# Key rows loaded plainly and transposed on TensorE, w1 loaded whole, and abs-max scans moved by one query block in a fused attention and MLP kernel

## Chip, cores and metric

One core of one Trainium2 chip. The metric is device time of one execution in microseconds (us). All arrays are bf16. Times are medians of several executions of a compiled kernel; the profile is a separate, recorded execution, whose span can differ from the median by some us.

## The reference, cut to what matters

```python
# x: [1, 2048, 576]; k_cache, v_cache: [1, 16, 2048, 128]; wq: [576, 4096]; wo: [4096, 576]
# w1, w2: [576, 576]; w3: [576, 4608]; w4: [4608, 576]
def reference(x, k_cache, v_cache, wq, wo, w1, w2, w3, w4):      # batch and head axes cut
    xn = layernorm(x)
    # attention: 32 query heads share 16 key heads, only the last W = 512 keys of 2048
    q = (xn @ wq) per head;  k, v = the last W keys and values, each used by two heads
    s = softmax(q @ k.T * 128**-0.5) @ v, heads joined, @ wo
    # gate branch on the same xn
    h  = gelu(layernorm(xn) @ w1)
    hs = (the four column quarters of h, shifted by +1, -1, +2, -2 rows) @ w2
    x1 = xn + hs
    g  = silu(x1 + gelu(layernorm(x1) @ w3) @ w4)
    return x + s * g
```

## The kernel before, the parts that matter

The attention part walks over 128 units, four query blocks of 512 rows times 32 heads, which the text calls block 0 to 3 and head 0 to 31. TensorE, the transfer issues on SyncE and the issues on GpSimd are in program order. In each unit TensorE gets the scores of this head, the query product of the next one, the value product of the one before, and a third at a time "atoms" of other work: gate-branch products (`b1` in heads 15 to 19, `b2` with the shifted `hs`) and the output product of the previous block. `at(u, ...)` hangs loads and VectorE work on a unit. The w3/w4 stage after unit 127 isn't touched.

```python
def load_kv(g, eng=None):          # keys are transposed on the way by the DMA, on SyncE's queue
    nc.sync.dma_start(out=kT[:, g, :], in_=A_k_cache[0, g, K0:, :], transpose=True)
    (eng or nc.gpsimd).dma_start(out=v_sb[:, g, :, 0:Dh],
        in_=A_v_cache[0, g, K0:, :].rearrange("(kc p) d -> p kc d", p=P))

def load_w1():                     # 4 x 4 = 16 issues on GpSimd
    for g in range(4):
        nc.gpsimd.dma_start(out=w1_sb[:, 0:NF, g * P:(g + 1) * P], ...)
        ...                        # cut: three more of this kind

def load_wo(i):                    # 4 loads of 1152 KB
    h0 = i * 8
    nc.gpsimd.dma_start(out=wo_sb[:, h0:h0 + 8, :], ...)

def transpose_tile(dstT, src, tt): # xnnT and xT_b are made by DMA transposes on SyncE's queue, too
    nc.sync.dma_start(out=dstT[:, :, tt * P:(tt + 1) * P], in_=src[:, tt, :], transpose=True)

def stage_t(u):                    # and so is oT, once per head, from one of 4 o buffers
    ...
    last_t[0] = nc.sync.dma_start(out=oT[:], in_=o[:].rearrange("p a b -> p (a b)"), transpose=True)

def gelu1(b, c, ph):               # VectorE steps of the gate's GELU; only the first has priority
    x = g1_pool.tile([P, QB], BF16, name="g_x")
    with tc.high_priority(offset=HP):
        nc.vector.tensor_copy(out=x[:], in_=ph[:, :])
    ...                            # cut: five more VectorE steps and a tanh on ScalarE

for b in range(NB):
    base = b * Hq
    later(base + 7, lambda b=b: ln2_steps(b), 3)                 # second layernorm -> xnn
    for tt in range(TB):
        at(base + 10 + tt, lambda b=b, tt=tt: tr2(b, tt))        # its 4 transposes -> xnnT
    for c in range(5):
        pe(base + 15 + c, b1(b, c))                              # needs xnnT
    ...
    if b + 1 < NB:
        later(base + 24, lambda b=b: ln1_steps(b + 1), 3)        # layernorm of the next block
        for tt in range(TB):
            at(base + 27 + tt // 2, lambda b=b, tt=tt: tr1(b + 1, tt))   # -> xT_b of the next block
at(2, lambda: late(..., load_w1))
for i in range(4):
    at(4 + 6 * i, lambda i=i: late(..., lambda: load_wo(i)))
for g in range(Hkv):
    if g + 3 < Hkv:
        at(2 * g + 1, lambda g=g: load_kv(g + 3))
for j in range(2, NB * 8):
    at(4 * (j - 1) - 1, lambda j=j: load_wq(j))                  # wq for four heads
for j in range(8):                                               # 40 abs-max scans, in block 1
    for kc in range(NDC):
        at(Hq + 4 * j + (kc + 1) // 2, lambda j=j, kc=kc: wq_max(j, kc))
```

Of the kernel before, what the change touches and what calls it, by code (L numbers as in the profile page):

```python
# [8 lines left out]
P = 128  # L9
# [20 lines left out]
def kernel(  # L30
# [131 lines left out]
    with ExitStack() as actx:  # L162
# [10 lines left out]
        w1_sb = res.tile([P, NDC, 5 * P], BF16, name="w1_sb")  # L173
# [39 lines left out]
        def load_kv(g, eng=None):  # L213
            nc.sync.dma_start(out=kT[:, g, :], in_=A_k_cache[0, g, K0:, :], transpose=True)
            (eng or nc.gpsimd).dma_start(out=v_sb[:, g, :, 0:Dh], in_=A_v_cache[0, g, K0:, :].rearrange("(kc p) d -> p kc d", p=P))
# [15 lines left out]
        with tc.manual_schedule(engines={SP}):  # L231
            load_wq(0, nc.sync)
            load_kv(0, nc.sync)
            load_kv(1, nc.sync)
            load_wq(1, nc.sync)
            load_kv(2, nc.sync)
        nc.gpsimd.memset(v_sb[:, :, :, Dh:VW], 1.0)
        nc.gpsimd.memset(w1_sb[:, :, 4 * P:], 0.0)
# [3 lines left out]
        def load_wo(i):  # L242
            h0 = i * 8
            nc.gpsimd.dma_start(out=wo_sb[:, h0:h0 + 8, :],
                                in_=A_wo[h0 * P:(h0 + 8) * P, :].rearrange("(h p) d -> p h d", p=P))

        def load_w1():
            for g in range(4):
                nc.gpsimd.dma_start(out=w1_sb[:, 0:NF, g * P:(g + 1) * P],
                                    in_=B_w1[0:NF * P, g * c4:g * c4 + P].rearrange("(kc p) m -> p kc m", p=P))  # L250
                nc.gpsimd.dma_start(out=w1_sb[0:DR, NF, g * P:(g + 1) * P],
                                    in_=B_w1[NF * P:D, g * c4:g * c4 + P])
                nc.gpsimd.dma_start(out=w1_sb[:, 0:NF, 4 * P + 32 * g:4 * P + 32 * g + rsz],
                                    in_=B_w1[0:NF * P, g * c4 + P:(g + 1) * c4].rearrange("(kc p) m -> p kc m", p=P))
                nc.gpsimd.dma_start(out=w1_sb[0:DR, NF, 4 * P + 32 * g:4 * P + 32 * g + rsz],
                                    in_=B_w1[NF * P:D, g * c4 + P:(g + 1) * c4])
# [140 lines left out]
        def b1(b, c):  # L397
            st = {}

            def mm(kc):  # L400
# [8 lines left out]
                nc.tensor.matmul(st["ph"][:, :], lhsT=w1_sb[:, kc, c * P:(c + 1) * P], rhs=xnnT[:, kc, :],  # L409
# [6 lines left out]
        def gelu1(b, c, ph):  # L416
            hb = hb_t[b]
            x = g1_pool.tile([P, QB], BF16, name="g_x")
            with tc.high_priority(offset=HP):
                nc.vector.tensor_copy(out=x[:], in_=ph[:, :])  # L420
# [67 lines left out]
        def finish_flag():  # L488
# [4 lines left out]
            m1 = small.tile([1, 2, P], FP32, name="m1", bufs=1)  # L493
            nc.gpsimd.dma_start(out=m1[:], in_=mx_dram[:, :].rearrange("(o p) c -> o c p", o=1))
            mm = small.tile([1, 2], FP32, name="mm", bufs=1)
            nc.vector.tensor_reduce(out=mm[:], in_=m1[:], axis=AX.X, op=ALU.max)
# [53 lines left out]
        for i in range(4):  # L550
            at(4 + 6 * i, lambda i=i: late(pT_t[4 + 6 * i][0][0:1, 0:1], lambda: load_wo(i)))
        at(Hq + 4, lambda: late(pT_t[Hq + 4][0][0:1, 0:1], load_w2))
        for g in range(Hkv):
            if g + 3 < Hkv:
                at(2 * g + 1, lambda g=g: load_kv(g + 3))
            at(Hq + 2 * g + 1, lambda g=g: k_max(g))
        for j in range(2, NB * 8):
            at(4 * (j - 1) - 1, lambda j=j: load_wq(j))
        for j in range(8):
            for kc in range(NDC):  # L560
                at(Hq + 4 * j + (kc + 1) // 2, lambda j=j, kc=kc: wq_max(j, kc))
# [3 lines left out]
        at(2 * Hq + 4, finish_flag)  # L565

        with tc.manual_schedule(engines={SP, POOL, PE}):
            for step in ln1_steps(0):
                step()
            for _ in range(2):  # L570
                wu = ps_sc.tile([P, QB], FP32, name="warm", tag="sc")
                for i in range(24):
                    nc.tensor.matmul(wu[:, 0:P], lhsT=ident[:, :], rhs=ident[:, :], start=True, stop=True)
# [266 lines left out]
```

## Time and profile before

| kernel before | |
|---|---|
| time, first timing | 886.71 us (886.49 to 887.57, 3 executions) |
| span of the profiled execution | 887.6 us |
| busy: TensorE, ScalarE, VectorE, GpSimd | 96%, 51%, 44%, 10% |
| block 0, 1, 2: first query to first query of the next | 119.6, 141.4, 133.8 us |
| first query of all | 13.9 us after the start |

How to read it: TensorE has hardly any idle time left, so the share of busy time says little. What says more is the rhythm of the heads. Undisturbed heads of block 0 start their query product every 2.88 us, those with five more gate products every 3.96 us. Whatever an interval is longer than that is lost, whether TensorE stood still or ran at a lower clock after it. The lines that carry this are in the prediction below.

### The profile page before, as it was taken

What the parts mean: (1) busy time and instruction counts of PE and PEld (TensorE: products, weight loads), DVE (VectorE), ACT (ScalarE), POOL (GpSimd) and SP (SyncE); (2) the same over time, 40 slices, a digit from 0 to 9 for tenths busy, and PEclk for the clock granted to TensorE, in tenths of its full rate; (3) what the DMA queues carried; (4) which work ended last, traced back from release to release, by engine and by line L of the source; (5) the groups of instructions that cost most, each with busy time, mean ns of one, the idle gap of its engine ahead of it and who ended that gap; (6) DMA issues with size and microseconds to landing.
All of it is one profiled execution on the core that took longest, in us unless ns stands there. A gap on an engine that the chain in (4) does not pass through costs nothing.

```text
span 887.6 us, 16225 instructions
## 1 busy us (share of the span) xinstructions
PE 853.2 (96%) x6460; PEld 473.6 (53%) x6460; DVE 387.7 (44%) x1201; ACT 455.2 (51%) x814; POOL 86.1 (10%) x148
## 2 busy tenths in 40 slices
PE   7896989999899999999999999999999999999996
PEld 4463555566455466565466565454444444444454
DVE  4584873258985135873125865300044007005033
ACT  2673774378777359877359876032233224225510
POOL 2722210211001021010001001000000000000000
PEclk7997999999999999999999999999999999999999
DMA  6698691246227146246127235990005004001001
GB/s 127 149 210 174 137 191 51 57 98 125 63 81 129 39 99 124 70 112 105 40 68 144 76 90 120 320 311 20 1 27 137 1 1 149 16 1 54 1 17 42
DMA packets 145873, 83.73 MB, mean 94 GB/s; under 512 B 113408, under 2 KB 139392, under 8 KB 145792
## 3 DMA queue, kind: packets, MB, share of 16 engines
q1 hardware_dynamic: 133840, 52.16, 27.9%
q0 software_dynamic: 8544, 27.23, 11.0%
q10 hardware_dynamic: 3408, 3.25, 1.1%
q8 instruction: 52, 0.85, 0.4%
q14 instruction: 29, 0.24, 0.1%
HBM read 47.07 MB, written 9.44 MB: 64 GB/s over the span
## 4 chain that ended last, share of the span: by engine, by line

## 5 line engine op out<-in xcount | busy, mean ns | idle before, releaser
L322 ACT ACTIVATE pT<-sc 128x512 bf16<-128x512 f32 x512 | 289.7, 596 | 122.8 <-PE sc L320 114.7
L320 PE MATMUL sc<-qT,kT 128*128 128x512 bf16 x512 | 184.2, 384 | 1.0 <-DVE qT L310 0.9
L645 PE MATMUL ph<-xT_b,w_s 128*128 128x512 bf16 x720 | 172.1, 379 | 0.0
L305 PE MATMUL psq<-xT_b,wq_b 128*128 128x512 bf16 x640 | 164.0, 388 | 7.4 <-DMA wq_b<-in_A_wq_dram 3.8
L337 PEld LDWEIGHTS <-pT 128*128 128x128 bf16 x2048 | 141.1, 98 | 53.9 <-issue 3.0
L648 ACT ACTIVATE h<-ph 128x512 bf16<-128x512 f32 x144 | 85.8, 597 | 155.4 <-PE ph L645 151.1
L337 PE MATMUL po<-v_sb,pT 128*128 128x129 bf16 x2048 | 163.4, 222 | 0.7 <-ACT pT L322 0.4
L654 PE MATMUL pm<-w_s,h 128*128 128x512 bf16 x540 | 145.8, 380 | 0.0
L665 DVE TENSOR_TENSOR bs<-pm,x 128x512 f32<-128x512 f32 (+3 forms) x18 | 11.1, 630 | 246.6 <-PE pm L654 198.6
L341 DVE RECIPROCAL ri<-po 128x2 f32<-128x2 f32 x256 | 42.5, 166 | 173.8 <-PE po L337 170.8
L361 PE MATMUL pswo<-wo_sb,oT 128*128 128x512 bf16 x512 | 116.5, 379 | 0.0
L342 DVE TENSOR_TENSOR o<-po,ri 128x256 bf16<-128x256 f32 x256 | 107.5, 420 | 6.7 <-DMA oT<-o 1.0
L305 PEld LDWEIGHTS <-wq_b 128*128 128x128 bf16 x640 | 63.1, 99 | 86.7 <-issue 11.4
L645 PEld LDWEIGHTS <-w_s 128*128 128x128 bf16 x720 | 63.8, 98 | 73.4
L655 PE MATMUL pr<-w_s,h 128*128 128x64 bf16 x540 | 99.1, 193 | 0.0
L361 PEld LDWEIGHTS <-oT 128*128 128x128 bf16 x1024 | 65.0, 98 | 55.1
L654 PEld LDWEIGHTS <-h 128*128 128x128 bf16 x540 | 52.7, 98 | 63.9 <-issue 0.6
L312 ACT ACTIVATE qT<-psq 128x512 bf16<-128x512 f32 x96 | 57.4, 598 | 32.5 <-PE psq L305 32.4
L320 PEld LDWEIGHTS <-kT 128*128 128x128 bf16 x512 | 47.6, 98 | 30.3 <-issue 3.2
L655 PEld LDWEIGHTS <-h 128*128 128x128 bf16 x540 | 51.0, 98 | 12.2 <-issue 0.4
L209 POOL DMA_DIRECT2D wq_b<-in_A_wq_dram x30 | 23.3, 778 | 327.2 <-PE psq L305 254.4
L409 PE MATMUL ph<-xnnT,w_sb 128*128 128x512 bf16 x100 | 32.5, 390 | 8.7 <-DMA xnnT<-xnn_b 8.7
(88 smaller groups left out, 472.4 us busy)
## 6 DMA issues: line engine op xcount, KB each, us to landing
wq_b<-in_A_wq_dram POOLq DMA_DIRECT2D x30, 512.0 KB, 4.9
w_s<-in_B_w_dram SPq DMA_DIRECT2D x9, 576.0 KB, 8.1
wo_sb<-in_A_wo_dram POOLq DMA_DIRECT2D x4, 1152.0 KB, 7.4
w_s<-in_B_w_dram SPq DMA_DIRECT2D x9, 512.0 KB, 9.3
x_dram<-x SPq DMA_DIRECT2D x4, 576.0 KB, 3.4
x<-x_dram SPq DMA_DIRECT2D x4, 576.0 KB, 4.7
s_b<-s_dram SPq DMA_DIRECT2D x4, 576.0 KB, 6.5
x_b<-in_A_x_dram SPq DMA_DIRECT2D x4, 576.0 KB, 6.2
```

Of the source, the lines that this page charges most:

```text
L305: nc.tensor.matmul(psq[:, :], lhsT=w[:, kc, hh * Dh:(hh + 1) * Dh], rhs=xT_b[qb % 2][:, kc, :], start=(kc == 0), stop=(kc == NDC - 1))
L312: nc.scalar.activation(out=qT[:, :], in_=psq[:, :], func=ACT.Copy)
L320: nc.tensor.matmul(sc[:, :], lhsT=kT[:, g, kc * P:(kc + 1) * P], rhs=qT_t[u][:, :], start=True, stop=True)
L322: nc.scalar.activation(out=pT[:, :], in_=sc[:, :], func=ACT.Exp, scale=SCALE)
L337: nc.tensor.matmul(po[:, j, :], lhsT=pTs[kc][:, tt * P:(tt + 1) * P], rhs=v_sb[:, g, kc, 0:Dh + 1], start=(kc == 0), stop=(kc == KCH - 1))
L341: nc.vector.reciprocal(out=ri[:], in_=po[:, :, Dh])
L342: nc.vector.tensor_tensor(out=o[:, t0:t0 + 2, :], in0=po[:, :, 0:Dh], in1=ri[:].unsqueeze(2).to_broadcast([P, 2, Dh]), op=ALU.mult)
L361: nc.tensor.matmul(ps, lhsT=oT_t[qb * Hq + h][:, tt, :], rhs=wo_sb[:, h, lo:hi], start=(h == 0), stop=(h == Hq - 1))
L645: nc.tensor.matmul(ph[:, :], lhsT=w3[:, kc, f0:f0 + P], rhs=xT_b[b % 2][:, kc, :], start=(kc == 0), stop=(kc == NDC - 1))
L648: nc.scalar.activation(out=h3[:, :], in_=ph[:, :], func=ACT.Gelu_apprx_tanh)
L654: nc.tensor.matmul(pm[tt][:, :], lhsT=lhsT, rhs=w4[:, fc % WS, 0:M0], start=(fc == 0), stop=(fc == FC - 1))
L655: nc.tensor.matmul(pr[:, tt, :], lhsT=lhsT, rhs=w4[:, fc % WS, M0:D], start=(fc == 0 and tt == 0), stop=(fc == FC - 1), skip_group_check=True)
```

## The change

Its intent is to take the waits out of block 0 and of the stretch of block 1 where VectorE is late.

- **Keys.** Four key heads come in one plain load. With key `4p + kc` on partition `p`, each partition reads 1 KB in one piece instead of 256 B rows. The values get the same order of keys, so the sum over the keys is unchanged. TensorE transposes them (4 instructions per key head into PSUM) and VectorE copies them out.
- **w1** comes in 2 issues instead of 16; four VectorE copies gather the odd columns later.
- **wo** comes in 8 loads of 576 KB instead of 4 of 1152 KB.
- **The 40 scans** of wq go from block 1 to block 2; all GELU steps of VectorE get priority.

```diff
-        def load_kv(g, eng=None):
-            nc.sync.dma_start(out=kT[:, g, :], in_=A_k_cache[0, g, K0:, :], transpose=True)
-            ...
+        def load_k(i, eng=None, step=4):
+            kst_t[i] = x1_pool.tile([P, TB, D], BF16, name="x1")
+            ...
+                    in_=A_k_cache[0, 4 * i + g:4 * i + g + step, K0:, :].rearrange("g (p kc) d -> p g (kc d)", p=P))
+        def prep_k(g):
+            ...
+                nc.tensor.transpose(out=st["ps"][:, kc * P:(kc + 1) * P], in_=src[:, kc * P:(kc + 1) * P],
+                                    identity=ident[:, :])
+                if kc == KCH - 1:
+                    with tc.high_priority(offset=HP):
+                        nc.vector.tensor_copy(out=kT[:, g, :], in_=st["ps"][:, :])
         def load_w1():
+            nc.gpsimd.dma_start(out=w1_sb[:, 0:NF, :], in_=B_w1[0:NF * P, :].rearrange("(kc p) m -> p kc m", p=P))
+            nc.gpsimd.dma_start(out=w1_sb[0:DR, NF, :], in_=B_w1[NF * P:D, :])
-            ...  (16 issues)
         def gelu1(b, c, ph):
+            with tc.high_priority(offset=HP):
+                gelu1_(b, c, ph)
-        for i in range(4):
-            at(4 + 6 * i, lambda i=i: late(pT_t[4 + 6 * i][0][0:1, 0:1], lambda: load_wo(i)))
+        at(10, gather_w1)
+        for i in range(8):
+            at(4 + 3 * i, lambda i=i: late(pT_t[4 + 3 * i][0][0:1, 0:1], lambda: load_wo(i)))
         ...
+        at(4, lambda: load_k(2))
+        at(12, lambda: load_k(3))
         for g in range(Hkv):
+            if g > 1:
+                pe_late.append((2 * g - 3, g))
         ...
-                at(Hq + 4 * j + (kc + 1) // 2, lambda j=j, kc=kc: wq_max(j, kc))
+                at(2 * Hq + 4 * j + (kc + 1) // 2, lambda j=j, kc=kc: wq_max(j, kc))
-        at(2 * Hq + 4, finish_flag)
+        at(3 * Hq + 4, finish_flag)
-            for _ in range(2):        # 48 warm-up products, now 32
         ...
+            for g in range(2):        # the first two key heads before the first query
+                for fn in prep_k(g):
+                    fn()
```

More of the change, by code (lines that the diff above doesn't have):

```diff
@@ L172 @@
         xnnT = res.tile([P, NDC, QB], BF16, name="xnnT")
-        w1_sb = res.tile([P, NDC, 5 * P], BF16, name="w1_sb")
+        w1_sb = res.tile([P, NDC, D], BF16, name="w1_sb")
+        w1r_sb = res.tile([P, NDC, P], BF16, name="w1r_sb")
         w2_sb = res.tile([P, 5, D], BF16, name="w2_sb")
@@ L211, in load_wq, with load_v, tr @@
             eng.dma_start(out=w[0:DR, NF, :], in_=A_wq[NF * P:D, c0:c0 + 4 * Dh])
-        def load_kv(g, eng=None):
-            nc.sync.dma_start(out=kT[:, g, :], in_=A_k_cache[0, g, K0:, :], transpose=True)
-            (eng or nc.gpsimd).dma_start(out=v_sb[:, g, :, 0:Dh], in_=A_v_cache[0, g, K0:, :].rearrange("(kc p) d -> p kc d", p=P))
+        kst_t = {}
+        def load_k(i, eng=None, step=4):
+            kst_t[i] = x1_pool.tile([P, TB, D], BF16, name="x1")
+            dst = kst_t[i][:].rearrange("p a b -> p (a b)")[:, 0:4 * W].rearrange("p (g a) -> p g a", g=4)
+            for g in range(0, 4, step):
+                (eng or nc.gpsimd).dma_start(
+                    out=dst[:, g:g + step, :],
+                    in_=A_k_cache[0, 4 * i + g:4 * i + g + step, K0:, :].rearrange("g (p kc) d -> p g (kc d)", p=P))
+        def load_v(i, eng=None):
+            for g in (2 * i, 2 * i + 1):
+                (eng or nc.gpsimd).dma_start(out=v_sb[:, g, :, 0:Dh],
+                                             in_=A_v_cache[0, g, K0:, :].rearrange("(p kc) d -> p kc d", p=P))
+        def prep_k(g):
+            st = {}
+            src = kst_t[g // 4][:].rearrange("p a b -> p (a b)")[:, (g % 4) * W:(g % 4 + 1) * W]
+            def tr(kc):
+                if kc == 0:
+                    st["ps"] = ps_wo.tile([P, W], BF16, name="ps_k", tag="wo")
+                nc.tensor.transpose(out=st["ps"][:, kc * P:(kc + 1) * P], in_=src[:, kc * P:(kc + 1) * P],
[3 more added lines that the diff above has]
+                        nc.vector.tensor_copy(out=kT[:, g, :], in_=st["ps"][:, :])
+            return [lambda kc=kc: tr(kc) for kc in range(KCH)]
         def late(ap, fn):
@@ L231 @@
         with tc.manual_schedule(engines={SP}):
+            load_k(0, nc.sync, 2)
             load_wq(0, nc.sync)
-            load_kv(0, nc.sync)
-            load_kv(1, nc.sync)
+            load_v(0, nc.sync)
             load_wq(1, nc.sync)
-            load_kv(2, nc.sync)
+            load_v(1, nc.sync)
+            load_k(1, nc.sync)
         nc.gpsimd.memset(v_sb[:, :, :, Dh:VW], 1.0)
-        nc.gpsimd.memset(w1_sb[:, :, 4 * P:], 0.0)
+        nc.gpsimd.memset(w1r_sb[:], 0.0)
         nc.gpsimd.memset(w1_sb[DR:, NF, :], 0.0)
@@ L242, in load_wo, with gather_w1 @@
         def load_wo(i):
-            h0 = i * 8
-            nc.gpsimd.dma_start(out=wo_sb[:, h0:h0 + 8, :],
-                                in_=A_wo[h0 * P:(h0 + 8) * P, :].rearrange("(h p) d -> p h d", p=P))
+            h0 = i * 4
+            nc.gpsimd.dma_start(out=wo_sb[:, h0:h0 + 4, :],
+                                in_=A_wo[h0 * P:(h0 + 4) * P, :].rearrange("(h p) d -> p h d", p=P))
         def load_w1():
+            nc.gpsimd.dma_start(out=w1_sb[:, 0:NF, :], in_=B_w1[0:NF * P, :].rearrange("(kc p) m -> p kc m", p=P))
+            nc.gpsimd.dma_start(out=w1_sb[0:DR, NF, :], in_=B_w1[NF * P:D, :])
+        def gather_w1():
             for g in range(4):
-                nc.gpsimd.dma_start(out=w1_sb[:, 0:NF, g * P:(g + 1) * P],
-                                    in_=B_w1[0:NF * P, g * c4:g * c4 + P].rearrange("(kc p) m -> p kc m", p=P))
-                nc.gpsimd.dma_start(out=w1_sb[0:DR, NF, g * P:(g + 1) * P],
-                                    in_=B_w1[NF * P:D, g * c4:g * c4 + P])
-                nc.gpsimd.dma_start(out=w1_sb[:, 0:NF, 4 * P + 32 * g:4 * P + 32 * g + rsz],
-                                    in_=B_w1[0:NF * P, g * c4 + P:(g + 1) * c4].rearrange("(kc p) m -> p kc m", p=P))
-                nc.gpsimd.dma_start(out=w1_sb[0:DR, NF, 4 * P + 32 * g:4 * P + 32 * g + rsz],
-                                    in_=B_w1[NF * P:D, g * c4 + P:(g + 1) * c4])
+                tc.keep_in_program_order(nc.vector.tensor_copy(
+                    out=w1r_sb[:, :, 32 * g:32 * g + rsz], in_=w1_sb[:, :, g * c4 + P:(g + 1) * c4]))
         def load_w2():
@@ L408, in mm @@
                     st["ph"] = ps_pq.tile([P, QB], FP32, name="ph", tag="pq")
-                nc.tensor.matmul(st["ph"][:, :], lhsT=w1_sb[:, kc, c * P:(c + 1) * P], rhs=xnnT[:, kc, :],
+                nc.tensor.matmul(st["ph"][:, :], rhs=xnnT[:, kc, :],
+                                 lhsT=w1r_sb[:, kc, :] if c == 4 else w1_sb[:, kc, c * c4:c * c4 + P],
                                  start=(kc == 0), stop=(kc == NDC - 1))
@@ L416, in gelu1, with gelu1_ @@
         def gelu1(b, c, ph):
+            with tc.high_priority(offset=HP):
+                gelu1_(b, c, ph)
+        def gelu1_(b, c, ph):
             hb = hb_t[b]
             x = g1_pool.tile([P, QB], BF16, name="g_x")
-            with tc.high_priority(offset=HP):
-                nc.vector.tensor_copy(out=x[:], in_=ph[:, :])
+            nc.vector.tensor_copy(out=x[:], in_=ph[:, :])
             u = g1_pool.tile([P, QB], BF16, name="g_u")
@@ L492, in finish_flag @@
             nc.gpsimd.dma_start(out=mx_dram[:, :], in_=m2[:])
-            m1 = small.tile([1, 2, P], FP32, name="m1", bufs=1)
-            nc.gpsimd.dma_start(out=m1[:], in_=mx_dram[:, :].rearrange("(o p) c -> o c p", o=1))
+            m1 = g1_pool.tile([P, QB], BF16, name="g_th")
+            m1 = m1[0:1, :].bitcast(FP32).rearrange("p (c n) -> p c n", c=2)
+            nc.gpsimd.dma_start(out=m1, in_=mx_dram[:, :].rearrange("(o p) c -> o c p", o=1))
             mm = small.tile([1, 2], FP32, name="mm", bufs=1)
-            nc.vector.tensor_reduce(out=mm[:], in_=m1[:], axis=AX.X, op=ALU.max)
+            nc.vector.tensor_reduce(out=mm[:], in_=m1, axis=AX.X, op=ALU.max)
             pr = small.tile([1, 1], FP32, name="pr", bufs=1)
@@ L549 @@
         at(2, lambda: late(pT_t[2][0][0:1, 0:1], load_w1))
-        for i in range(4):
-            at(4 + 6 * i, lambda i=i: late(pT_t[4 + 6 * i][0][0:1, 0:1], lambda: load_wo(i)))
+        at(10, gather_w1)
+        for i in range(8):
+            at(4 + 3 * i, lambda i=i: late(pT_t[4 + 3 * i][0][0:1, 0:1], lambda: load_wo(i)))
         at(Hq + 4, lambda: late(pT_t[Hq + 4][0][0:1, 0:1], load_w2))
+        pe_late = []
+        at(4, lambda: load_k(2))
+        at(12, lambda: load_k(3))
         for g in range(Hkv):
-            if g + 3 < Hkv:
-                at(2 * g + 1, lambda g=g: load_kv(g + 3))
+            if g % 2 == 0 and g >= 4:
+                at(2 * g - 8, lambda g=g: load_v(g // 2))
+            if g > 1:
+                pe_late.append((2 * g - 3, g))
             at(Hq + 2 * g + 1, lambda g=g: k_max(g))
@@ L569 @@
                 step()
-            for _ in range(2):
-                wu = ps_sc.tile([P, QB], FP32, name="warm", tag="sc")
-                for i in range(24):
-                    nc.tensor.matmul(wu[:, 0:P], lhsT=ident[:, :], rhs=ident[:, :], start=True, stop=True)
+            wu = ps_sc.tile([P, QB], FP32, name="warm", tag="sc")
+            for i in range(32):
+                nc.tensor.matmul(wu[:, 0:P], lhsT=ident[:, :], rhs=ident[:, :], start=True, stop=True)
+            for g in range(2):
+                for fn in prep_k(g):
+                    fn()
             tr1_first()
@@ L576 @@
             for u in range(0, max(max(fill), max(pe_fill)) + 1):
-                atoms = pe_fill.get(u, [])
+                atoms = pe_fill.get(u, []) + [fn for v, g in pe_late if v == u for fn in prep_k(g)]
                 n = len(atoms)
```

## The prediction

> **What bounds the kernel now.** I read the page first, then the waits of TensorE alone, then tables of stretches, then the timeline around each wait.
>
> ```profile
> PE 853.2 (96%) x6460; PEld 473.6 (53%) x6460; DVE 387.7 (44%) x1201; ACT 455.2 (51%) x814; POOL 86.1 (10%) x148
> ...
> PE   7896989999899999999999999999999999999996
> ...
> PEclk7997999999999999999999999999999999999999
> ```
>
> TensorE is busy 96% of the span, and the rest, 34.4 us, is mostly in the first seven of the 40 slices (22.2 us each). The granted clock dips in the same slices. So the kernel is TensorE-bound, and what a change of loads can give back lies in query block 0 (heads 0 to 31) and the seam to block 1. The waits of TensorE name the gaps (total, times, longest):
>
> ```profile
> PE ph L409 <- DMA xnnT<-xnn_b: 8.7, 2, 8.5
> PE psq L305 <- DMA wq_b<-in_A_wq_dram: 3.8, 1, 3.8
> PE psq L305 <- DMA xT_b<-xn_b: 3.7, 2, 3.3
> ...
> PE psx L456 <- DVE hs L445: 2.8, 1, 2.8
> ```
>
> Stretches by block (PE, PEld, DVE, ACT, POOL busy, clock, DMA share, GB/s), then 5 us pieces around the first two gaps:
>
> ```profile
> 17.00:133.00 116.00, 100.63 (x785) 59.20 (x784) 75.90 (x239) 73.42 (x130) 36.63 (x58) 0.92 0.79 164
> 133.00:275.00 142.00, 138.02 (x1122) 80.67 (x1123) 92.95 (x280) 92.27 (x170) 17.15 (x30) 0.98 0.37 86
> 275.00:410.00 135.00, 135.00 (x1128) 79.64 (x1128) 65.93 (x229) 92.72 (x172) 14.77 (x24) 1.00 0.43 92
> ```
>
> ```profile
> 40.00:45.00 5.00, 2.51 (x6) 0.89 (x7) 0.16 (x1) 0.00 (x0) 2.52 (x4) 0.67 0.99 301
> ...
> 70.00:75.00 5.00, 0.00 (x0) 0.00 (x0) 0.16 (x1) 0.00 (x0) 0.24 (x1) 0.74 1.11 255
> 75.00:80.00 5.00, 2.75 (x13) 1.61 (x14) 0.60 (x2) 0.60 (x1) 0.00 (x0) 0.50 0.83 120
> 80.00:85.00 5.00, 5.00 (x31) 2.47 (x29) 2.99 (x8) 2.37 (x5) 2.22 (x4) 0.73 0.22 41
> ```
>
> Each gap is paid twice: the wait, and half clock after it. To get both as one number I took the start of each head's first query matmul from the timeline. Undisturbed heads of block 0 follow each other in 2.88 us, those with five more gate-branch matmuls in 3.96. Against that: head 8 came 3.9 us late and head 9 another 1.3 (**A**, wq, 5.2); the head with the wait for xnnT took 14.71 instead of 3.96 and the next 0.6 to 1 more (**B**, 11.8); head 32 was 3.5 late and the next 1.65 (**C**, xT, 5.1); in block 1 the heads at the wait for hs lost 2.9 and 1.65, two later ones 1.1 (**D**, 5.7). The first heads lost some 1.5 to a cold clock. Check: block 1 took 141.4 us from its first query matmul to block 2's, block 2 with the same TensorE work 133.8; the 7.6 us between them is D plus the 1.65 of C.
>
> Why the waits arise: A is GpSimd's issue queue.
>
> ```profile
> 25.44 0.75 POOL L249 DMA_DIRECT2D w_sb<-in_B_w_dram  x1
> ...
> 35.35 0.54 POOL L255 DMA_DIRECT2D w_sb<-in_B_w_dram  x1
> 35.89 0.78 POOL L215 DMA_DIRECT2D v_sb<-in_A_v_cache_dram  x1
> 36.66 0.75 POOL L209 DMA_DIRECT2D wq_b<-in_A_wq_dram  x1
> ```
>
> Sixteen w1 pieces take 10.4 us to issue; the wq load stands behind them and lands at 42.5. B is SyncE's in-order queue of transposes plus full DMA engines:
>
> ```profile
> 56.28 1.74 SPq L271 DMA_TRANSPOSE xnnT<-xnn_b  x1
> ...
> 61.82 3.17 SPq L214 DMA_TRANSPOSE kT<-in_A_k_cache_dram  x1
> 65.09 1.22 SPq L350 DMA_TRANSPOSE oT<-o  x1
> ...
> 68.99 1.29 SPq L271 DMA_TRANSPOSE xnnT<-xnn_b  x1
> ```
>
> The fourth xnnT issues 12.7 us after the first and lands 8 us later, at 77.2. D is VectorE working off abs-max scans (0.67 us each) between the GELU steps that make hs.
>
> **What the Trainium skill says.** "TensorE: Matmul & The Clock Gate", Part 1, says that the clock is judged in free-running windows of about 3.4 us and that an idle one halves it; the clock column (0.50 at 75 to 80) agrees. Part 4 of that page gives 275 to 390 ns for a TensorE transpose and says that it lands in PSUM and needs a copy; the trace disagrees on the size, eight of them took 1.01 us at the start (126 ns each, at half clock). "DMA: Bandwidth & Descriptors", Issuing engines are not separate DMA queues, says that all queues share the same 16 DMA engines; the trace agrees, the DMA share stands at 0.83 to 1.11 from 45 to 80. Its Specifications table asks for 512 B or more per transfer for line rate; in the page 113,408 of 145,873 packets are smaller, which are the transposes, and of which the keys are 16 of about 190 issues.
>
> **The change part by part.**
>
> A. w1 becomes 2 issues. The wq load is then issued about 9 us earlier (14 x 0.65), some 28 us, and needs 5 to 6 us to land: 34, against a need at 38.7. The wait goes, with its cold clock: -5.2.
>
> B. Sixteen kT transposes leave SyncE's queue (1.26 us each, up to 3.2). Between the first and the last xnnT there are then six issues in place of seven before the last. But GpSimd now issues more bulk in that stretch: by my count of the program order 576 KB of wo per three heads, the wq loads, 512 KB of keys at head 12, values in pairs at head 12, 576 KB of x at head 14: about 2.9 MB in five heads, and SyncE's 4 xnnT and 5 oT go beside it. At the 210 GB/s that 40 to 80 us shows, 4.1 MB need 19 us and five heads last 15. The xnn tiles are also not ready sooner: VectorE's order puts two of four before head 11's query copy, as now. Last issue near 63, landing 5 to 8 later, need at 65.5: I expect 4 us of wait left and 1.7 of cold clock in place of 11.8: -6.
>
> C. The xn tiles of block 1 come at the same place in VectorE's order or two thirds of a head later. Fewer transposes are in flight then. I leave 3 of 5.1: -2.
>
> D. The 40 wq scans (26.0 us) leave block 1, and the GELU chain gets priority: -5 of 5.7. Block 2 has VectorE at 65.9 of 135 us, so 26 us fit (92 of 135, as in block 1 now), but its order has up to three scans among the GELU steps before hs: +1. Together -4.
>
> E. Added: 64 TensorE transposes. Eight run before the first query, 56 in the stream of heads, which has no slack: at full clock half of 126 ns, about 60 ns: 56 x 0.06 = +3.4.
>
> F. Start: the first two key transposes share one PSUM buffer, and VectorE copies them only after the four layernorm applies (which end at 11.3 now). Copy 0.42, four cold transposes 0.45, then the x transposes, which start at 10.3 now: first query at about 15.2 instead of 14.0: +1.2. Sixteen warm-up matmuls less lie in idle time: 0.
>
> G. VectorE gets 16 copies of 0.42 us and four small gathers in block 0, 7.3 us on top of 75.9 of 116 us. From 85 to 130 us it is busy 39.4 of 45, so it runs late there sometimes: +0.7.
>
> Sum: -5.2 - 6 - 2 - 4 + 3.4 + 1.2 + 0.7 = -11.9, so 886.7 - 11.9 = 874.8, about 875.
>
> **Rivals.** (1) All four waits vanish. For it: every part aims at one of them, and the kT issues and the 1152 KB bursts of wo are cut. Then the gain is 27.8 - 5.3 = 22.5: 864. Against it: the byte count above, and C's place in VectorE's order. (2) xnnT stays as late, because DMA bandwidth and not SyncE's issue holds it, and VectorE's extra copies push xn later so that C grows by 2: gain 5.2 + 4 - 2, cost 5.3: 885. For it: the DMA share of about 1.0; the keys still move the same bytes. (3) VectorE becomes the bound in the second half of block 0: heads 15 to 31 need 1.86 us each for query and output copies, 0.42 for every second head's key, 12.7 for GELU and 7.8 for the layernorm: 54 us, against 53 of TensorE. Then query and PSUM copies slip and each head costs 0.2 to 0.3 more, +3 to +5: about 879.
>
> **Range and chances.** A is nearly sure, D likely, B decides. B between 0 and 11.8 left gives 869 to 881, C and G add some 2 either way: 868 to 883. Over 2% faster means under 869, which needs nearly all of rival 1: 0.13. Slower by 2% would need a new wait of some 30 us: 0.02.
>
> **What would show it.** A right: no wait of psq for wq_b. B: the wait of ph for xnnT between 2 and 6 us; none would speak for rival 1, over 7 for rival 2. C: the wait of psq for xT_b at 2 to 3. D: no wait for hs in block 1, and block 1 within 2 us of 133.8. E: plain heads of block 0 with a key transpose 0.2 to 0.25 longer than 2.88; more would show the transpose or its copy on the path. F: first query near 15.2. I am wrong if TensorE waits for the key copies or if the loads of keys or values land after their heads.

## The result, and the profile after

| | before | after |
|---|---|---|
| median of 4 executions, us | 887.14 (886.49 to 887.81) | 874.76 (873.81 to 875.72) |
| ratio, 95% interval | | 0.986 (0.9843 to 0.9878) |
| profiled span, us | 887.6 | 872.1 |
| block 0, 1, 2, us | 119.6, 141.4, 133.8 | 106.8, 135.8, 134.5 |

Ratios are the mean time of one kernel's runs over that of the other's in the same rounds, so not quite the ratio of the medians quoted. Executions over 1.5% slower than the fastest of the same kernel are left out of the means. All runs in this document were correct. The kernel became 1.4% faster, within the 2% band, and the time predicted was 875.0.

The page of the kernel after; the second and third line are tenths in 40 slices, now of 21.8 us:

```profile
PE 841.3 (96%) x6393; PEld 473.9 (54%) x6508; DVE 394.0 (45%) x1221; ACT 454.7 (52%) x814; POOL 80.5 (9%) x143
...
PE   5999979999999999999999999999999999999996
...
PEclk9999989999999999999999999999999999999999
```

The dips of the second, fourth and eleventh slice (A, B and D of the prediction) are gone. The first is lower, 5 instead of 7: there are 16 fewer warm-up products (3.6 us of them instead of 5.3), and the first query comes later. The sixth, from 109 to 131 us, is the seam from block 0 to block 1, and it stays. The TensorE sum must not be compared with before's: this trace lacks records of some query and score matmuls (602 of 640 and 494 of 512). I therefore took each head's start from its first query weight load, all of which are there.

The waits of TensorE, in the kernel after:

```profile
PE psq L332 <- issue: 5.3, 1, 5.3
PE ps_k L237 <- DVE kT L241: 4.7, 1, 4.7
PE ph L436 <- issue: 1.8, 1, 1.8
...
PE ph L436 <- DMA xnnT<-xnn_b: 0.5, 1, 0.5
...
PE psx L487 <- DVE hs L476: 0.2, 1, 0.2
```

No wait for wq_b, 0.2 for hs. The 4.7 for the key copy lie before the first query. "Issue" means that the profile names no releaser; the timeline below shows that the 5.3 of psq are the wait for xT_b. The 1.8 of ph lies at the first gate product of block 3, which starts at 473.3; the last xnnT there issued at 467.0, and the longest of its four landings took 6.2 us, which ends at 473.2. So this is a wait for xnnT.

The first stretch of the kernel after, with the same columns as in the prediction:

```profile
17.00:133.00 116.00, 108.30 (x898) 67.21 (x913) 84.28 (x268) 79.89 (x142) 30.54 (x52) 0.97 0.77 162
```

TensorE is busy 7.7 us more at 0.97 instead of 0.92 of the clock (the same microseconds now hold more of the program), while the DMA share and the rate (0.77, 162 GB/s) hardly differ from before. The transfers weren't made lighter on average; they were put in another order.

Where the time went, as time lost over the undisturbed rhythm (us, from the heads' starts; 2.88, 3.96 with gate products, and 0.22 more where a key head is transposed). "After, again" is the unaltered kernel in a later execution.

| place | term of the prediction | before | after | after, again | predicted |
|---|---|---|---|---|---|
| start of the first query | F | 13.9 | 14.85 | 14.9 | +1.2 |
| heads 0 to 2 | (none) | 1.4 | -0.4 | 1.6 | |
| heads 3 to 15 | A | 5.2 | 0 | 0 | -5.2 |
| key transposes, 14 x 0.22 | E | 0 | 3.1 | 3.1 | +3.4 |
| heads 16 to 30 | B | 11.8 | 1.0 | 2.5 | -6 |
| seam to block 1 | C | 5.1 | 7.5 | 6.8 | -2 |
| rest of block 1 | D | 5.4 | -0.1 | -0.1 | -5 |
| block 2 with its seam | D | 0.4 | 0.8 | 0.8 | +1 |
| block 3 | (none) | 0.3 | 1.9 | 0 | |
| late VectorE | G | | 0 in the heads; see C | | +0.7 |

The differences of the column "after" sum to -14.9 us and those of the second execution to -13.9; the spans differ by 15.5 and 14.0 (872.1 and 873.6 against 887.6). So the table accounts for the result within 1 us. It also shows that the good match of the total has two errors in it: B gave 3.3 to 4.8 us more than predicted, C took 3.7 to 4.4 more.

A, in GpSimd's timeline of the kernel after:

```profile
24.69 0.75 POOL L277 DMA_DIRECT2D w_sb<-in_B_w_dram  x1
...
25.96 0.78 POOL L210 DMA_DIRECT2D wq_b<-in_A_wq_dram  x1
```

The load of wq is issued at 25.96 instead of 36.66. B and C, on SyncE's queue and TensorE of the kernel after:

```profile
51.94 1.20 SPq L298 DMA_TRANSPOSE xnnT<-xnn_b  x1
...
59.91 1.30 SPq L298 DMA_TRANSPOSE xnnT<-xnn_b  x1
...
108.86 3.57 SPq L298 DMA_TRANSPOSE xT_b<-xn_b  x2
...
113.84 2.54 SPq L298 DMA_TRANSPOSE xT_b<-xn_b  x2
...
121.72 2.29 PE L332 MATMUL psq<-xT_b,wq_b 128*128 128x512 bf16 x5 [5.25 <-issue]
```

The four xnnT now issue within 8.0 us instead of 12.7, and the last one 2.2 us before the query of head 16 starts, where it had been 2.4 us after it. The first gate product has its turn 2.1 us after that start, at 64.2; the last xnnT landed at 64.6, 4.7 us after its issue, and that leaves the wait of 0.5. For C, the same view of the kernel before:

```profile
122.41 2.52 SPq L271 DMA_TRANSPOSE xT_b<-xn_b  x2
...
126.34 3.59 SPq L271 DMA_TRANSPOSE xT_b<-xn_b  x2
...
133.57 2.04 PE L305 MATMUL psq<-xT_b,wq_b 128*128 128x512 bf16 x5 [3.33 <-DMA xT_b<-xn_b]
```

The queries of head 32 could run without waiting at 129.9 before (the time when the query's turn would have come) and at 116.1 after. Measured from there, the xn tiles ended at -5.8 before and -5.2 after, the last xT_b issued at -2.2 and -0.9 (second of the two in the lines at 126.34 and 113.84), and all had landed at +3.7 and +5.6. So VectorE was 0.6 us later, the queue of SyncE 0.7 more, and the flight (from issue to landing) took 0.6 more. But the flight of the last xT_b was long in both kernels, 5.8 us before and 6.5 after; the experiments come back to it.

### The profile page after: what moved, and what is told of

The parts are those of the page before. It is cut to its first block, busy times and chain, and to the rows that moved or that the text cites. A ratio compares the mean times of both kernels' runs of the same rounds, so it can differ in the third digit from the quotient of the medians.

```text
span 872.1 us, 16198 instructions
## 1 busy us (share of the span) xinstructions
PE 841.3 (96%) x6393; PEld 473.9 (54%) x6508; DVE 394.0 (45%) x1221; ACT 454.7 (52%) x814; POOL 80.5 (9%) x143
## 2 busy tenths in 40 slices
DMA packets 138675, 83.75 MB, mean 96 GB/s; under 512 B 105072, under 2 KB 131952, under 8 KB 138592
## 4 chain that ended last, share of the span: by engine, by line
## 5 line engine op out<-in xcount | busy, mean ns | idle before, releaser
L347 PE MATMUL sc<-qT,kT 128*128 128x512 bf16 x494 | 176.1, 379 | 1.6 <-DVE qT L337 0.8
L332 PE MATMUL psq<-xT_b,wq_b 128*128 128x512 bf16 x602 | 153.3, 382 | 7.3 <-issue 5.3
L694 PE MATMUL pm<-w_s,h 128*128 128x512 bf16 x523 | 143.3, 380 | 0.1
L388 PE MATMUL pswo<-wo_sb,oT 128*128 128x512 bf16 x497 | 114.2, 379 | 0.8
L398 ACT ACTIVATE s_out<-pswo 128x512 bf16<-128x512 f32 x16 | 9.6, 597 | 48.2 <-PE pswo L388 48.2
```

The source lines that it names most:

```text
L332: nc.tensor.matmul(psq[:, :], lhsT=w[:, kc, hh * Dh:(hh + 1) * Dh], rhs=xT_b[qb % 2][:, kc, :], start=(kc == 0), stop=(kc == NDC - 1))
L347: nc.tensor.matmul(sc[:, :], lhsT=kT[:, g, kc * P:(kc + 1) * P], rhs=qT_t[u][:, :], start=True, stop=True)
L388: nc.tensor.matmul(ps, lhsT=oT_t[qb * Hq + h][:, tt, :], rhs=wo_sb[:, h, lo:hi], start=(h == 0), stop=(h == Hq - 1))
L694: nc.tensor.matmul(pm[tt][:, :], lhsT=lhsT, rhs=w4[:, fc % WS, 0:M0], start=(fc == 0), stop=(fc == FC - 1))
```

## The experiments

My first theory was: A is GpSimd's issue time; B went because the backlog of bulk loads, with w1 and wq some 10 us earlier, is worked off sooner; C grew because the layernorm of the next block comes too late in program order; D is VectorE's order. The main rivals: B went because SyncE's queue, freed of the key transposes, lets xnnT through; C is a collision with a wq load in flight; D was cured by the priority of the GELU steps and not by moving the scans. Twelve kernels ran, from 3 to 5 rounds each. On these chips the kernel before had medians of 885.9 to 886.2 us, over a wider range than at first (881.8 to 892.4), so single differences below some 3 us are left undecided by the times; the heads' rhythm in the profile is finer.

**b_w1_whole**: the kernel before with only the w1 part.

```diff
 # on the kernel before
-    w1 in 16 pieces
+    nc.gpsimd.dma_start(out=w1_sb[:, 0:NF, :], in_=B_w1[0:NF * P, :].rearrange("(kc p) m -> p kc m", p=P))
+    nc.gpsimd.dma_start(out=w1_sb[0:DR, NF, :], in_=B_w1[NF * P:D, :])
+    at(10, gather_w1)
```

> The kernel before, with w1 loaded whole by two issues and its remainder columns gathered by VectorE; nothing else changed. Theory 1 (backlog): the sixteen w1 issues hold up not only the wq load (wait A, 5.2 us with its cold clock) but push all bulk loads of block 0 into the stretch in which xnnT moves, so that wait B (11.8 us) shrinks with A: 10 to 16 us faster than before, 871 to 877, with little or no wait for xnnT. Rival (SyncE): B comes from the sixteen key transposes in SyncE's queue and stays at 8 to 11 us: only A goes, 5 us faster, about 882. Either way waits C (seam to block 1) and D (hs) stay, and heads without a gate matmul stay at 2.88 us.

Measured: 882.4 us (879.2 to 885.9), ratio 0.9956 (0.9904 to 1.0008), so not clear of noise. The wait for wq at head 8 is gone, but heads 3 to 15 still lose 7.1 us, now at head 12, and heads 16 to 30 lose 3.2 instead of 11.8. Its waits of TensorE:

```profile
PE po L336 <- DVE o L341: 4.4, 2, 4.2
PE psx L456 <- DVE hs L445: 2.8, 1, 2.8
PE ph L408 <- DMA xnnT<-xnn_b: 2.3, 1, 2.3
```

and what VectorE waited for there, in its timeline:

```profile
50.57 0.42 DVE L341 TENSOR_TENSOR o<-po,ri 128x256 bf16<-128x256 f32 x1 [5.50 <-DMA oT<-o]
```

The four o buffers were all waiting for their transposes out. So the loads that now start earlier seem to hold up the transposes of oT instead; while TensorE waits there, the xnnT catch up. Neither theory had this (the rival's 882 is met, but not its B of 8 to 11): A and B together went from 17.0 to 10.3, and a wait taken away came back at another place.

**a_w1_pieces**: the change without the w1 part.

```diff
 # on the kernel after
-    w1 in 2 issues, gather_w1 at head 10
+    w1 in 16 pieces again
```

> The changed kernel with w1 loaded in sixteen pieces again. Theory (A is GpSimd's issue time): the wq load for head 8 is issued 9 us later, wait A returns with 3 to 4 us and its cold clock 1.3, and the bulk loads behind it bunch up beside xnnT, so that B grows by 0 to 5: 5 to 10 us slower than the changed kernel, 880 to 885. Rival (the keys and halved wo bursts had removed A): 1 us slower at most.

Measured: 878.8 us (875.7 to 881.5), ratio 0.9919 (0.9865 to 0.9972); the unaltered kernel after had 875.0 on this chip. Heads 3 to 15 lose 4.6 us again, and the wait has its old name:

```profile
PE psq L333 <- DMA wq_b<-in_A_wq_dram: 2.7, 2, 1.8
```

So with the other parts in place, the w1 part is worth 4.6 us in the rhythm and some 4 in the time (where the intervals of the two ratios overlap), a bit less than the 5 expected.

**a_keys_dmat**: the change without the keys part.

```diff
 # on the kernel after
-    load_k, load_v, prep_k
+    nc.sync.dma_start(out=kT[:, g, :], in_=A_k_cache[0, g, K0:, :], transpose=True)
+    at(2 * g + 1, lambda g=g: load_kv(g + 3))
```

> The changed kernel with the keys put back: DMA transposes on SyncE, one key group at a time, values in the old key order, no key transposes on TensorE, no key copies on VectorE; w1 whole, wo in eighths and the scans in block 2 stay. Theory 1 (backlog from w1 made B): the wait for xnnT stays at 0 to 2 us, heads fall to 2.88 us each (-3.1), first query 0.9 earlier, wait C falls from 7.5 to about 5 because VectorE has no key copies: 869 to 873, that is faster than the changed kernel by 2 to 6. Rival (SyncE made B): B comes back by 5 to 10: 877 to 884.

Measured: 872.2 us (869.0 to 876.9), ratio 0.9836 (0.978 to 0.9893). B is back at 10.0 us:

```profile
PE ph L409 <- DMA xnnT<-xnn_b: 7.4, 1, 7.4
```

It is not only SyncE's issues that are late. The last xnnT issued 0.2 us ahead of its need, instead of 2.2. Their landings, first in this kernel and then in the kernel after, both from the view of this tile between 40 and 80 us:

```profile
DMA to landing us min/median/max: 5.4/6.4/9.6
```

```profile
DMA to landing us min/median/max: 4.7/4.8/6.6
```

So my first theory of B falls, and the rival holds: the key transposes, with the order of the value loads that came back with them, made most of B, by 2 us of issue and by 1.6 (median) to 3 us (longest) of landing. But the time isn't worse: E's 3.1 us and F's 0.9 are saved, and the seam lost 0.3 instead of 7. Taken alone the keys part doesn't pay.

The seam of this run says more about C than its size. Without the key part the xn tiles end 5.8 us and the last xT_b (second of this line) issues 2.2 us before the turn of head 32:

```profile
119.27 2.55 SPq L271 DMA_TRANSPOSE xT_b<-xn_b  x2
```

These are to 0.1 us the times of the kernel before. There the last xT_b was in flight for 5.8 us (its issue took 1.0 us longer), and the seam lost 5.1; here it is 2.6 us, and the seam loses 0.3. So the place of the layernorm doesn't settle C by itself: the flight does as much. The key part, in turn, makes VectorE 0.6 us and the last issue 1.3 us later.

**a_ln1_early**: the layernorm and the transposes for block 1 three heads earlier.

```diff
 # on the kernel after
-                later(base + 24, lambda b=b: ln1_steps(b + 1), 3)
+                e = 3 if b == 0 else 0
+                later(base + 24 - e, lambda b=b: ln1_steps(b + 1), 3)
-                    at(base + 27 + tt // 2, lambda b=b, tt=tt: tr1(b + 1, tt))
+                    at(base + 27 - e + tt // 2, lambda b=b, tt=tt: tr1(b + 1, tt))
```

> The changed kernel with the layernorm of block 1's x and its DMA transposes three heads earlier in block 0 (heads 21 to 25 in place of 24 to 28). Theory: wait C (5.6 us and 1.9 of cold clock at head 32) is VectorE's lateness plus transposes that start only 7.6 us before they are needed; with three heads (8.9 us) more it goes altogether: 7 us faster than the changed kernel, about 868. Rival: the wait at head 32 is for the wq load or for DMA bandwidth at that place and stays above 3 us: 873 to 875; or VectorE, pressed between GELU and layernorm at heads 21 to 24, holds up query copies and the gain shrinks to 3.

**a_wq9_late**: the wq load closest to the seam two heads later.

```diff
 # on the kernel after
-            at(4 * (j - 1) - 1, lambda j=j: load_wq(j))
+            at(4 * (j - 1) - 1 + (2 if j == 9 else 0), lambda j=j: load_wq(j))
```

> The changed kernel with one wq load (the one for heads 36 to 39, needed some 30 us later) issued two heads later, so that it does not move beside the last two transposes of xT for block 1. Theory (DMA contention makes half of C): the transposes land about 2 us sooner after their issue and wait C falls from 7.5 to 4 or 5: about 872. Rival (only VectorE's and SyncE's order make C): within 1 us of the changed kernel, 874 to 875.

Measured: 871.6 us (868.0 to 873.7), ratio 0.9814 (0.977 to 0.9858) for the first; 877.7 (875.1 to 882.7), ratio 0.9916 (0.9866 to 0.9965) for the second. With the earlier layernorm the seam loses 0.0 instead of 7.5: all xT_b have landed 2.5 us before the turn of head 32. The second run still loses 7.0, but its edit didn't move the load. In the kernel after and in a_wq9_late it issues as follows:

```profile
114.75 0.78 POOL L210 DMA_DIRECT2D wq_b<-in_A_wq_dram  x1 [10.43 <-PE psq L332]
```

```profile
118.13 0.78 POOL L210 DMA_DIRECT2D wq_b<-in_A_wq_dram  x1 [10.43 <-PE psq L332]
```

Both are 1.3 us before the turn of head 32 (116.1 and 119.5), because the load waits for the query products that still read its buffer, and not for its place in the program. So a_wq9_late is the kernel after once more, its 877.7 us show the spread, and the rival, a collision with this load, stays untested by a run. The traces speak for it. In the kernel after, the third xT_b issues 0.9 us before this load and lands after 2.6 us; the fourth issues 0.4 us after it and lands after 6.5. In the trace's records of single packets SyncE's queue starts none from 115.97 to 117.96, while GpSimd's queue moves 418 KB; before, after_again, a_wq9_late and a_keys_dmat show such a stop of 1.6 to 2.2 us at the same place, and in a_keys_dmat the xT_b were through by then. So C is, as far as the record shows, an issue that comes too late to get ahead of the wq load; a_ln1_early shows the cure, and not which of the two is the cause.

The profile of a_ln1_early still lost 4.8 us at the xnnT in block 0 and 4.9 in block 2, where its program is the same as after's:

```profile
PE ph L436 <- DMA xnnT<-xnn_b: 5.6, 2, 3.1
```

**after_again**: the kernel after once more, unaltered, to see how much of that is chance.

> The changed kernel again, unaltered, for its own spread on this chip. If the 0.9 us of wait B in its first profile was chance, as the 2.2 and 4.6 us of two kernels with the same program up to head 16 suggest, B lies anywhere from 0 to 5 here; wait C, 5.4 to 5.6 us with 1.4 to 1.9 of cold clock in both kernels that keep it, should be there again; the first three heads take 8.5 or 10 us[...]. Ratio to the kernel before 0.984 to 0.989.

Measured: 875.0 us (874.1 to 881.1), ratio 0.9881 (0.9838 to 0.9924); profiled span 873.6. Heads 16 to 30 lost 2.5 us and the seam 6.8. Up to the first of these heads the programs of after, after_again, a_ln1_early, a_wq9_late and a_scans_b1 (below) are the same, and B was 1.0, 2.5, 4.8, 2.2 and 1.1. What is left of B is a wait on transfers that ends differently in each execution, 2.3 us in the mean.

**a_early**: also the second layernorm and its transposes four heads earlier.

```diff
 # on a_ln1_early
-            later(base + 7, lambda b=b: ln2_steps(b), 3)
+            later(base + 3, lambda b=b: ln2_steps(b), 3)
-                at(base + 10 + tt, lambda b=b, tt=tt: tr2(b, tt))
+                at(base + 6 + tt, lambda b=b, tt=tt: tr2(b, tt))
```

> The changed kernel with both block-0 layernorm chains earlier: xnn and its transposes four heads earlier (in all blocks), xn of block 1 and its transposes three heads earlier. Theory (the two remaining waits are lateness of VectorE and SyncE's order, not bandwidth): no wait for xnnT in any block, none at head 32, heads otherwise unchanged; 8 to 11 us faster than the changed kernel, 864 to 866, ratio to before 0.974 to 0.978. Rival (DMA bandwidth bounds block 0): the bulk loads then run late in another place, a wait of 3 us or more appears for wq, keys or values, and the gain is 3 to 6.

**a_keys_dmat_early**: the same two shifts, with the DMA transposes for the keys.

```diff
 # on a_keys_dmat: the shifts of a_ln1_early and a_early
```

> The same two shifts with the keys by DMA transposes on SyncE, as in a_keys_dmat. Once no wait is left, the key part of the change should cost what its instructions cost: 14 heads without 0.22 us of transposes (-3.1) and the first query 0.9 earlier, so 4 us faster than a_early if SyncE's queue has room (860 to 862). Rival (the key transposes on SyncE do harm of their own by filling its ring): xnnT or oT land late, a wait for xnnT, wq or the o buffers of 4 us or more shows in block 0, and it is no faster than a_early.

Measured: 872.6 us (868.7 to 880.1), ratio 0.985 (0.9802 to 0.9899), and 865.6 (863.4 to 871.2), ratio 0.977 (0.9727 to 0.9813). In the first, no wait for xnnT or xT_b is left, but heads 3 to 15 lose 9.4 and heads 16 to 30 lose 3.2. The wait and its cause, in the waits of TensorE and the timeline of VectorE of a_early:

```profile
PE po L364 <- DVE o L369: 10.3, 4, 6.9
```

```profile
68.81 0.42 DVE L369 TENSOR_TENSOR o<-po,ri 128x256 bf16<-128x256 f32 x1 [8.54 <-DMA oT<-o]
```

It is the wait of b_w1_whole once more: the o buffers aren't free, since the transposes of oT don't get through. The earlier xnnT passed the wait on to the next transposes in the same queue. In a_keys_dmat_early, heads 3 to 30 lose 6.6 in place of 12.6.

**a_wo_late**: the loads of wo, which block 1 is the first to use, out of heads 4 to 15.

```diff
 # on the kernel after
-            at(4 + 3 * i, lambda i=i: late(pT_t[4 + 3 * i][0][0:1, 0:1], lambda: load_wo(i)))
+            at(16 + 2 * i, lambda i=i: late(pT_t[16 + 2 * i][0][0:1, 0:1], lambda: load_wo(i)))
```

> The changed kernel with the eight loads of wo, which nothing needs before head 33, issued at heads 16 to 30 (every second head) in place of 4 to 25 (every third); nothing else. Theory (bandwidth in heads 4 to 16 makes B): 2.4 MB fewer move before head 16, so wait B (2.5 us in the second profile) is 0; wait C (5.4 and 1.5) stays or grows by 1 to 3, because more bulk moves at heads 26 to 30: 873 to 877, about the same. Rival (B is only SyncE's and VectorE's order): B stays at 1 to 4.

Measured: 873.8 us (868.7 to 879.8), ratio 0.9842 (0.9798 to 0.9886). B is 0.0, the seam loses 8.4, and this profile lost 4.5 at the xnnT of block 2. This points to the bulk loads of heads 4 to 15 as what was left of B; wo is the part of them with slack. It is one profile, in which the last xnnT landed only 0.4 us before its need, against 1.0 at best in five without the shift. The time didn't move beyond its spread.

**a_early_wo_late** and **k_early_wo_late**: all three shifts together, with the keys by TensorE and by DMA.

```diff
 # on a_early and on a_keys_dmat_early: the edit of a_wo_late
```

> The changed kernel with both layernorm chains earlier and wo later. Theory (a_early moved wait B onto the o buffers because the DMA engines were full at heads 10 to 15): with wo out of that stretch no wait of TensorE over 1 us is left in block 0 after the first heads, head 32 in time: q of head 32 about 103 us after the first; 5 to 8 us faster than a_early, 865 to 867. Rival: the o buffers still hold TensorE up by 3 us or more, since it is the transposes' own packets that are slow; 870 to 873.

> The same with the keys by DMA transposes on SyncE. If no wait is left in both, the difference is what key transposes on TensorE cost: 3.1 us in the heads and 0.9 at the start, so 861 to 863, 3 to 5 us faster than a_early_wo_late. Rival (key transposes on SyncE fill its ring): a wait for o or xnnT of 4 us or more remains here and not there, and the two are level within 2 us.

Measured: 864.7 us (864.0 to 866.1), ratio 0.975 (0.9721 to 0.978), and 865.6 (861.8 to 867.5), ratio 0.9748 (0.9709 to 0.9786). The longest wait of TensorE in a_early_wo_late, before the first query (the next are 1.6 at the warm-up products, 1.1 for the key load and 0.8 for a query copy):

```profile
PE ps_k L237 <- DVE kT L241: 5.0, 1, 5.0
```

None over 0.5 us is for xnnT, xT_b, wq_b, hs or o. Its block 0, in the table of stretches:

```profile
17.00:117.00 100.00, 98.42 (x824) 61.09 (x837) 78.67 (x254) 71.79 (x128) 29.37 (x50) 0.97 0.75 168
```

TensorE is busy 98.4 of 100 us at the same DMA share as after. Block 0 takes 102.3 us, and nothing is lost in heads 3 to 31, the seam or block 1. This version beats both kernels: its interval lies below after's (0.9843 to 0.9878, in other rounds). In k_early_wo_late block 0 takes 98.7, 3.6 less: about 1.9 of it from the first three heads, which differ by chance, and the rest from saved transposes less 1.4 lost. That profile then lost 5.2 at the seam to block 3 with

```profile
PE psq L305 <- issue: 3.8, 3, 3.4
```

which, by the landing of xT_b there, is C at a later block: the xn tiles end 8.5 us before the need, as in the kernel after, but the last xT_b issues 1.7 us before it instead of 2.9 and is in flight for 5.4 us instead of 2.7, again beside a wq load. Only block 1's layernorm had been moved. The two times are level.

**a_scans_b1**: the scans back in block 1, the priority of the GELU steps kept.

```diff
 # on the kernel after
-                at(2 * Hq + 4 * j + (kc + 1) // 2, lambda j=j, kc=kc: wq_max(j, kc))
+                at(Hq + 4 * j + (kc + 1) // 2, lambda j=j, kc=kc: wq_max(j, kc))
```

> The changed kernel with the 40 wq scans back in block 1 and the flag at its old place; the GELU steps keep their high priority. Theory (the scans make D): the wait for hs returns with 2 to 3 us and 1.65 of cold clock, block 1 takes 139 to 141 in place of 135.7 and block 2 133.8 in place of 134.5: 4 us slower, 878 to 880. Rival (the priority of the GELU steps cured D): no wait for hs over 1 us, and level with the changed kernel within 1 us.

(The flag that reads the scans' result stayed where the change had put it, contrary to that text; it reads the result later than the text says and nothing else.) Measured: 878.3 us (875.5 to 879.6), ratio 0.9902 (0.9869 to 0.9934). The waits of TensorE:

```profile
PE psq L332 <- DMA xT_b<-xn_b: 2.0, 1, 2.0
...
PE psx L487 <- DVE hs L476: 1.0, 1, 1.0
```

The wait for hs is 1.0 instead of 2.8, with no lower clock after it, so the rest of block 1 loses 1.4 instead of 5.4. But the seam to block 2 loses 2.2: with 26 us more on VectorE the xn tiles for block 2 end 7.3 us before the need instead of 9.4 in the kernel after, and the last xT_b is in flight for 4.9 us instead of 3.1. So the priority took most of D, moving the scans took the rest and kept that seam free. For the priority this is by elimination: no run takes it alone away; w1 is not the cause, since b_w1_whole still waits 2.8 us for hs, but the keys and wo parts changed along with it. I had counted both as one.

## Why the prediction was right or wrong

The predicted total was off by 0.2 us; its range held. Point by point:

- **The bound** was right: TensorE, with the loss in block 0 and at the seam. So was the accounting by head starts, in which each wait is paid a second time in clock.
- **A** was right: -5.2 predicted and shown, with the mechanism confirmed by a_w1_pieces (4.6 back). The issue came at 25.96, earlier than "some 28 us". What the prediction didn't see is that alone, on the kernel before, this part moves the loss instead: 7.1 us came up at head 12, where the oT transposes were late. A and B together gave 6.7 us in the rhythm and 3.6 in the median, not clear of noise (b_w1_whole).
- **B** is the first mis-sized term: -6 predicted, -9.3 and -10.8 in the two profiles. The failed step is "Last issue near 63, landing 5 to 8 later, need at 65.5": the last issue was at 59.9, it landed after 4.7 us, and the first gate product had its turn at 64.2, so 0.5 us of wait were left and not 4. Counting "six issues in place of seven" on SyncE weighed the number of issues and not the time: a key transpose beside bulk loads took up to 3.2 us of the queue and slowed the landing of the others (a_keys_dmat). The byte count itself may not be wrong in kind: 1.0 to 4.8 us remained, and in the one profile of a_wo_late, with fewer bytes there, none.
- **C** is the second: "I leave 3 of 5.1", because "fewer transposes are in flight then"; 7.5 and 6.8 were lost. The step that failed is the shorter flight: without the key transposes in SyncE's queue the last xT_b took 6.5 us to land instead of 5.8. Besides, VectorE ended the xn tiles 0.6 us later, SyncE its issues 1.3 later, and 1.9 later all had landed. The prediction had the delay in its hands as "two thirds of a head later" and as G, but booked it elsewhere and at 0.7. Three heads earlier the loss is gone (a_ln1_early); with the same issue time as before and a flight of 2.6 us it is gone, too (a_keys_dmat). What makes the flight long was not tested; the packets point to the wq load.
- **D** was right in its sum: -5.5 in block 1 (-5 predicted), and block 2 lost 0.4 more (+1 predicted). Its cause was split differently from what the text says.
- **E and F** were right: 14 x 0.22 = 3.1 (3.4 predicted), so 55 ns per transpose; first query 0.9 to 1.0 later (1.2 predicted). Apart from C, neither the transposes nor their copies were on the path beyond this.
- **G**: no plain head was longer. It shows in C alone.
- **Rivals.** Neither (1), which B and A resembled, nor (2), whose C was right (it said that copies push xn later and C grows by 2; it grew by 1.7 and 2.4, and without the key part xn ended 0.6 us earlier) and whose B was wrong, nor (3), of which nothing is seen. The wait of ph for xnnT, "none would speak for rival 1", was 0.5 in the first profile: this sign pointed to a rival that the total didn't follow, because C hid it.
- **What no term held**: the first three heads lose -0.6 to 1.9 us by execution in either way of loading keys, and losses of up to 4.9 us at the xnnT come up in blocks 2 and 3 in some executions. That the spread of the times follows from such waits is not shown: a_early_wo_late, which has none, had the tightest times of the twelve, but the kernel after in its first timing (873.8 to 875.7) was as tight with them.
- **Two readings of lines.** Of the 113,408 small packets 101,888 are transposes; most others are words of 4 B and rows of values. The DMA share from 45 to 80 went up to 1.15 (at 60 to 65), and not 1.11.

That -6 and -2 should have been about -10 and +2 cancels to within the spread, so the total is right for a reason that is partly luck.

Open: what exactly holds up the transposes while bulk loads run. For B the runs point to the loads (a_wo_late, one profile) and the key transposes (a_keys_dmat). The packet records show GpSimd's queue going ahead of SyncE's in bursts (in the kernel before, from 72 to 74 us, 561 KB against 18), but not by what rule. A run that really moves the wq load at the seam is missing.

## What to carry to other kernels

Where TensorE is full, read the rhythm of the repeated unit and not the waits: it also counts the lower clock after a wait, and the sum of what is lost by place can be checked against the time. A load that gets through earlier can hold up whatever runs at that time, so a removed wait is worth its size only if nothing behind it is short of the same thing: first move the bulk loads with slack (here wo, not used for a whole block) out of the crowded stretch, then move producers such as the layernorm earlier in program order. Replacing DMA transposes by TensorE ones costs what TensorE takes (here 3 us and 1 at the start) and paid no more than that here, once the waits were removed in the cheaper way. After a run that is to move a transfer, look in its trace whether the transfer moved (a_wq9_late): one that waits for its buffer doesn't follow its place in the program.

## What the Trainium skill lacked or had wrong

- "TensorE: Matmul & The Clock Gate", Part 4, gives about 275 to 390 ns for a TensorE transpose. In the stream of heads four of them lengthened a head by 0.22 us, 55 ns each, and eight at the start of the kernel before took 126 ns each at half clock; the trace gives each of the 64 for the keys 218 ns (median, with a modelled end). The page's value taken for the cost in a full stream would give an estimate of 15 to 22 us (56 transposes) instead of 3.1.
- "DMA: Bandwidth & Descriptors", Issuing engines are not separate DMA queues, says that the time to issue is usually small relative to the transfer. Here it was not: 16 small pieces of w1, which landed 2.4 to 3.3 us (medians) after their issue, took 10.4 us of issue on GpSimd, and two whole loads moved the next load's issue from 36.66 to 25.96.
- The same section says that all transfers interleave on the same engines, which the runs agree with; no page has a figure for what this does to small transposes beside bulk loads: SyncE's queue started no packet for 2.0 us at the seam of the kernel after, xnnT took 4.7 to 6.6 us to land in the kernel after, 5.4 to 9.6 with key transposes beside them, and the resulting wait of TensorE differed between executions of one program from 1.0 to 4.8 us.
- The Specifications table of that page asks for at least 512 B per transfer for line rate, and this isn't wrong here: in the first 14 us of the kernel after, before any DMA transpose, SyncE's packets of 256 B took 22 ns (median, 11.6 B per ns) and those of 1,024 B 46 ns (22 B per ns). But it didn't decide the result: with 105,072 packets under 512 B instead of 113,408, the stretch from 17 to 133 us moved 162 instead of 164 GB/s.
